# A fused hashed-attention and gated feed-forward kernel: the first head prepared in two mixed parts, a new order for the first batch, and a last output row in three parts

## The chip, the cores and the metric

The kernel runs on one core of a Trainium2 chip. The metric is the device time of one execution in microseconds (us); three executions of the kernel before the change are given, and one further execution was recorded by the profiler. A difference under 0.2% cannot be told from no change here.

## The reference

Batch 4, 8 heads, 768 positions, head width 64; q, k, v are float32. `proj` is 64x6: a position's bucket is the sign pattern of six projections.

```python
q_bits = (einsum('bhsd,dk->bhsk', q, proj) > 0); k_bits = the same of k
mask   = q_bucket[:, :, :, None] == k_bucket[:, :, None, :]
scores = where(mask, q @ k.T / sqrt(64), -1e9)
attn   = softmax(scores);  x = (attn @ v), heads side by side: 3072 x 512
g, val = x @ w_gate, x @ w_val                       # 512 x 1536 each
out    = x + sigmoid(x @ w_res) * ((gelu(g) * val) @ w_out)
```

## The kernel before, in words

The mask becomes part of the matmul. Every row of q and k (64 numbers) gets six bits (plus or minus a half) and a constant behind it, 71 numbers in all, so that one product of 71-number rows gives a score that the exponential turns to nothing where the buckets differ.

A *pair* is two heads; there are 16 pairs, four in each batch, and a batch ends with its feed-forward stage. 768 positions are six tiles of 128 (T = 6), so that a pair has twelve tiles of q and twelve of k. What one side of a pair goes through, with the short names of the lists:

- `ld`: q or k arrives by a DMA that SyncE issues (`lv`: v). The first head's q and k are loaded by themselves (L125), q0, k0, q1, k1; the rest of the first loads follow in the order FIRST_LOADS.
- `tr` (L240): VectorE transposes the float32 data in blocks of 32.
- `h` (L251; for the first pair `hoq`, `ho`, L293): TensorE multiplies by `proj`, in float32.
- `tk`, `bt` (L266, L282; for the first pair `bits_one`, L299 and L301): VectorE turns the sums back and writes the six bits into `nat`, in the bfloat16 rows that are to be transposed. For side 1 (k) of pairs 1 to 3 GpSimd does half of the four writes.
- `cs` (L208, L210): GpSimd copies q (scaled) or k into the first 64 columns of `nat`. There are four `nat` buffers, so a buffer is filled again only when the pair before the last has been transposed.
- `tp` (L320) and `td` (L329): TensorE transposes a head's six tiles into PSUM and VectorE copies them to `aug`, which the scores read. From pair 4 on `tu` (L308) does both by a transposing DMA.

The digits are pair, side (0 for q, 1 for k) and head: `td201` copies the second head of q of pair 2. On the attention side `s<n>` (L448, L459) is a unit of scores: two PSUM banks of 512 columns by TensorE and one exponential of 1024 columns on ScalarE; a pair has nine units, the fifth of which ends the first head and begins the second. `v<n>` (L421) multiplies unit n's exponentials by v, and a head ends with a small product, `preset` (L393), which adds a tiny multiple of the sum of v over the tiles, so that rows without a match come out as a mean. That sum is `vs` (L346 to L350, GpSimd), and `va` (L338) is v in bfloat16. `fin` (L372, L373) divides on VectorE and writes x. Scores have two PSUM buffers (`sc_ps`), values two (`av_ps`), and two banks serve the rest.

Batch 0's attention has no feed-forward work beside it; its 36 units and everything around them stand in a list by hand, ORDER, in which each engine takes its instructions in turn and waits for the data of the one in front. The weights of the feed-forward stage arrive by DMAs that GpSimd issues (`w0` to `w11`, L193: gate and value columns in quarters, then `w_res`, then `w_out` in thirds).

Then comes `gate_val` of batch 0: for each of twelve blocks m, eight matmuls for the gate and eight for the value (L472), a Gelu on ScalarE (L489) and a product on VectorE (L492, "hh"); BESIDE names what is issued behind block m's product: the preparation of batch 1. The gate's PSUM buffer is free when the Gelu has read it, the value's when the product has. Batches 1 to 3 follow a fixed plan by slots, with the feed-forward output (`project`, L504 to L526) between the scores. Before all this TensorE multiplies zeros (`fill`, L174) until data has come. At the very end `project` computes the last 128 rows: four matmuls for the residual gate, then the output columns in two parts, 384 columns and 128, each with twelve matmuls (L518), two VectorE steps (L521, L524) and a store (L526).

Of the kernel before, what the change touches and what calls it, by code (L numbers as in the profile page):

```python
# [16 lines left out]
FIRST_LOADS = [(1, "q"), (0, "v"), (1, "k"), (2, "q"), (2, "k"), (1, "v"), (2, "v"), (3, "k"), (3, "q")]  # L17
# [29 lines left out]
def kernel(  # L47
# [12 lines left out]
    nc = tc.nc  # L60
# [99 lines left out]
    for i in range(NN):  # L160
        blank(i, nc.vector)

# [48 lines left out]

    t32, hsum, htok = {}, {}, {}
# [23 lines left out]
    def tr(p, side, h0=0, h1=2):  # L236
        if (p, side) not in t32:
            t32[p, side] = t32_pool.tile([P, HT, 2, 32], FP32, tag="t32", name="t32")
        sl = slice(h0 * T, h1 * T)
        nc.vector.transpose(t32[p, side][:, sl].rearrange("p c h n -> p (c h n)"),  # L240
                            raw[p, side][:, sl].rearrange("p c d -> p (c d)"))

# [53 lines left out]

    def bits_one(p, side, hi):
        hs = hsum.pop((p, side, hi))
        nc.vector.transpose(hs[:, 1].rearrange("p c n -> p (c n)"),  # L299
                            hs[:, 0].rearrange("p c n -> p (c n)"))  # L300
        nc.vector.tensor_scalar(nat_of((p, side))[:, hi * T:hi * T + T, D:D + NBITS],  # L301
                                hs[:, 1, :, 0:NBITS], 0.0, 0.5, op0=ALU.is_gt, op1=ALU.subtract)
        acc_done(("hs", p, side, hi))
# [19 lines left out]
    def turned(p, side, hi, eng, t0=0, t1=T):  # L323
# [6 lines left out]
        if t1 == T:  # L330
            give((p, side, hi))
            if ("pt", p, side, hi) in accs:
                acc_done(("pt", p, side, hi))

# [163 lines left out]
    def project(b):  # L498
        hh = hidden[b]
        for t in range(T):  # L500
# [41 lines left out]
    bits_one(0, 1, 0)  # L542
    turned(0, 0, 0, nc.scalar, 0, 4)
    turn_pe(0, 1, 0)
    turned(0, 1, 0, nc.vector, 0, 2)
# [79 lines left out]
    job("tdk", lambda: turned(0, 1, 0, nc.vector, 2, T))  # L625
    job("tdq", lambda: turned(0, 0, 0, nc.vector, 4, T))
# [150 lines left out]
```

## Time and profile before

| | |
|---|---|
| three executions | 345.9, 346.1, 346.1 us (median 346.1) |
| the profiled execution | 346.07 us, of which the span of the trace is 344.4 us |
| mean granted TensorE clock | 0.998 |
| TensorE matmul busy | 333.5 us (97%) |
| VectorE, ScalarE, GpSimd busy | 191.7, 206.2, 85.6 us |
| first exponential starts, last one of batch 0 ends | 8.50 us, 46.9 us |
| batch 1's first score unit | 82.44 us |
| last VectorE step ends | 341.0 us |

Times in the views are microseconds from the start of the span. A timeline row has the start, the length, the engine, the line of the kernel, the operation, the tile written and the tile read with their shapes, and how many like instructions were merged ("x6"); in brackets stands how long the engine had been idle and what it waited for. PE is TensorE, DVE VectorE, ACT ScalarE, POOL GpSimd, and SPq the queue of DMAs that SyncE issues.

### The profile page before, as it was taken

The page shows a single profiled execution, that of the slowest core. Times are in us where ns is not written, and L with a number is a line of the kernel's source. Part 1 is how long each engine was busy: PE and PEld are TensorE (multiplying, and loading weights), DVE is VectorE, ACT ScalarE, POOL GpSimd, SP SyncE. Part 2 cuts the span into 40 slices and gives each one's busy share as a digit, 9 for nine tenths or more (in the row PEclk, how much of TensorE's full clock was granted, in tenths as well). Part 3 has the DMA queues.
Part 4 walks back from the last instruction along what each step waited for, and adds up shares of the span by engine and source line. Part 5 has one row for each costly group of instructions (what it writes and reads, how often), then busy time and mean ns, then how long its engine had stood idle before and what let it go on. Part 6 is the DMA issues. An engine that isn't in the chain of part 4 may idle for free.

```text
span 344.4 us, 7546 instructions
## 1 busy us (share of the span) xinstructions
PE 333.5 (97%) x3064; PEld 204.3 (59%) x3112; DVE 191.7 (56%) x404; ACT 206.2 (60%) x232; POOL 85.6 (25%) x162
## 2 busy tenths in 40 slices
PE   8998999999999999999999999999999999999994
PEld 4675766555666655655666665656566665566442
DVE  6979737656344856757344784747244444343333
ACT  3888972226999962224999982223999984223110
POOL 3887920317055000260043200242030000000000
PEclk9999999999999999999999999999999999999999
DMA  7959998999976743528366642725430220000022
GB/s 215 376 128 280 146 241 149 181 127 176 189 175 188 210 107 78 101 39 148 82 194 188 227 115 65 131 49 109 75 100 32 55 55 30 33 0 0 32 79 75
DMA packets 71171, 42.90 MB, mean 125 GB/s; under 512 B 49504, under 2 KB 68192, under 8 KB 71136
## 3 DMA queue, kind: packets, MB, share of 16 engines
q1 hardware_dynamic: 64720, 37.17, 44.0%
q0 software_dynamic: 6336, 5.24, 10.2%
q8 instruction: 24, 0.39, 0.5%
q14 instruction: 11, 0.09, 0.1%
q10 hardware_dynamic: 80, 0.00, 0.0%
HBM read 29.36 MB, written 6.29 MB: 104 GB/s over the span
## 4 chain that ended last, share of the span: by engine, by line
PE 90%; DVE 3%; ACT 3%; issue 1%; DMA 1%; SPq 0%; POOL 0%; DVEq 0%; ACTq 0%; POOLq 0%
PE sp L472 34%; PE fps L518 18%; PE sp L448 17%; PE av L421 9%; PE rps L504 6%; PE hs L251 3%; ACT hh L459 2%; DMA ld<-in_k_dram 1%; PE pt L320 1%; PE wps L174 1%; DVE nat L282 1%; PE hs L293 1%; DVE aug L329 1%; ACT gt L489 0%; SPq L308 0%
## 5 line engine op out<-in xcount | busy, mean ns | idle before, releaser
L459 ACT ACTIVATE e<-sp 128x1024 bf16<-128x1024 f32 x108 | 109.0, 1028 | 8.0 <-PE sp L448 2.8
L489 ACT ACTIVATE gt<-sp 128x768 bf16<-128x768 f32 x48 | 38.9, 810 | 92.8 <-PE sp L472 92.8
L448 PE MATMUL sp<-aug,aug 71*128 71x256 bf16 (+1 forms) x384 | 85.8, 325 | 2.0 <-DVE aug L329 1.6
L518 PE MATMUL fps<-wo,hh 128*128 128x512 bf16 (+2 forms) x275 | 74.6, 369 | 1.4
L492 DVE TENSOR_TENSOR hh<-gt,sp 128x768 bf16<-128x768 bf16 x48 | 45.7, 953 | 48.0 <-PE sp L472 43.9
L472 PE MATMUL sp<-x_sb,wv 128*128 128x256 bf16 (+1 forms) x378 | 70.6, 325 | 0.7 <-DVE hh L492 0.4
L472 PE MATMUL sp<-x_sb,wg 128*128 128x256 bf16 (+1 forms) x373 | 70.4, 324 | 0.7
L421 PEld LDWEIGHTS <-e 128*128 128x128 bf16 x864 | 40.2, 97 | 25.1
L472 PEld LDWEIGHTS <-wv 128*128 128x128 bf16 x384 | 37.6, 98 | 25.3 <-issue 0.6
L472 PEld LDWEIGHTS <-wg 128*128 128x128 bf16 x384 | 36.7, 98 | 26.0 <-issue 2.3
L421 PE MATMUL av<-va,e 128*128 128x65 bf16 x864 | 43.4, 193 | 0.0
L518 PEld LDWEIGHTS <-hh 128*128 128x128 bf16 x300 | 27.4, 97 | 22.5
L459 ACT ACTIVATE hh<-sp 128x1024 bf16<-128x1024 f32 x36 | 34.4, 1026 | 5.1 <-PE sp L448 5.0
L521 DVE SCALAR_TENSOR_TENSOR o<-th,fps 128x512 f32<-128x512 f32 (+2 forms) x25 | 16.7, 666 | 36.9 <-PE fps L518 30.0
L448 PEld LDWEIGHTS <-aug 71*128 71x128 bf16 x384 | 29.2, 97 | 13.0 <-issue 2.0
L346 POOL TENSOR_TENSOR v<-ldv 128x384 f32<-128x384 f32 x16 | 16.0, 999 | 64.1 <-DMA ldv<-in_v_dram 64.0
L240 DVE STREAM_TRANSPOSE t<-ld 128x768 f32<-128x768 f32 (+1 forms) x34 | 30.5, 912 | 1.6 <-DMA ld<-in_k_dram 1.4
L400 DVE COPY av<-av 128x390 f32<-128x390 f32 x24 | 13.6, 567 | 29.7 <-PE av L396 29.7
L208 POOL TENSOR_SCALAR nat<-ld 128x768 bf16<-128x768 f32 (+1 forms) x16 | 13.8, 860 | 60.1 <-DMA aug<-nat 55.4
L504 PE MATMUL rps<-wr,x_sb 128*128 128x512 bf16 x90 | 25.6, 378 | 0.3
L508 ACT ACTIVATE th<-rps 128x512 f32<-128x512 f32 x24 | 14.3, 594 | 18.5 <-PE rps L504 18.5
L210 POOL CAST nat<-ld 128x768 bf16<-128x768 f32 (+1 forms) x17 | 13.3, 783 | 39.7 <-DMA aug<-nat 38.8
(64 smaller groups left out, 242.5 us busy)
## 6 DMA issues: line engine op xcount, KB each, us to landing
ldv<-in_v_dram SPq DMA_DIRECT2D x16, 384.0 KB, 5.4
out_dram<-o SPq DMA_DIRECT2D x23, 256.0 KB, 2.0
ld<-in_q_dram SPq DMA_DIRECT2D x15, 384.0 KB, 5.6
ld<-in_k_dram SPq DMA_DIRECT2D x15, 384.0 KB, 5.2
wg<-in_moe_w_gate_dram POOLq DMA_DIRECT2D x4, 384.0 KB, 8.5
wv<-in_moe_w_val_dram POOLq DMA_DIRECT2D x4, 384.0 KB, 9.0
wo<-in_moe_w_out_dram POOLq DMA_DIRECT2D x3, 512.0 KB, 9.4
wr<-in_moe_w_res_dram POOLq DMA_DIRECT2D x1, 512.0 KB, 7.7
```

Source lines behind the costliest of these rows:

```text
L240: nc.vector.transpose(t32[p, side][:, sl].rearrange("p c h n -> p (c h n)"), raw[p, side][:, sl].rearrange("p c d -> p (c d)"))
L346: nc.gpsimd.tensor_add(v3, vs[:, :, 0:3, :], vs[:, :, 3:6, :])
L421: nc.tensor.matmul(av[p, hi][:, qt, :], e[:, off:off + P], va[:, hi, jt, 0:D + 1], start=first, stop=(p >= HP and jt == T - 1), skip_group ...
L448: nc.tensor.matmul(sp[:, off:off + nq * P], ks[0:KA, hi * T + jt, :], qs[0:KA, hi * T + qt0:hi * T + qt0 + nq, :], start=True, stop=True)
L459: nc.scalar.activation(e, sp, AF.Exp, scale=float(ALPHA))
L472: nc.tensor.matmul(sp[:, c0:c1], w[:, kk, bass.ts(m, P)], xs[:, kk, c0:c1], start=(kk == 0), stop=(kk == KM - 1))
L489: nc.scalar.activation(gt, sp[:, 0:S], AF.Gelu)
L492: nc.vector.tensor_mul(hidden[b][:, m, :], gt, ps[1][:, 0:S])
L504: nc.tensor.matmul(rps, x_sb[b][:, kk, t, :], wr[:, kk, :], start=(kk == 0), stop=(kk == KM - 1))
L508: nc.scalar.activation(th, rps, AF.Tanh, scale=0.5)
L518: nc.tensor.matmul(fps[:, cs], hh[:, m, bass.ts(t, P)], wo[:, m, cs], start=(m == 0), stop=(m == KF - 1))
L521: nc.vector.scalar_tensor_tensor(o[:, cs], th[:, cs], 1.0, fps[:, cs], op0=ALU.add, op1=ALU.mult)
```

## The change

Three edits. First, the first head is no longer prepared as "q, then k" but as two parts: part 0 has tiles 0 to 3 of q and tiles 0 and 1 of k (what the first score unit reads), part 1 the other two tiles of q and four of k. Each part has a load for each side, a `t32` tile, a hash bank, one `bits_one` for both its sides, and rows of its own in a new tile `lead`; `PARTS` lists (side, first tile, end); `load_part` issues one DMA of those tiles and `turned_part` copies as `turned` does. `tpB` transposes part 1 (into a values bank), `tdk` and `tdq` copy it. The multiplications by zero are cut from 7 x 512 + 256 + 2 x 256 columns to 6 x 512 + 128, and VectorE makes two of the four copies of `proj`. Second, FIRST_LOADS, ORDER and BESIDE stand in a new order. Third, the last rows' output columns go in three parts, 256, 128 and 128, the last in a values bank.

```diff
-FIRST_LOADS = [(1, "q"), (0, "v"), (1, "k"), (2, "q"), (2, "k"), (1, "v"), (2, "v"), (3, "k"), (3, "q")]
+FIRST_LOADS = [(1, "q"), (0, "v"), (1, "k"), (2, "q"), (2, "k"), (2, "v"), (3, "q"), (1, "v"), (3, "k")]
...
 ORDER = """
-trq trk s0 tdq tdk hoq bo0 ho bo1 s1 tr10 s2 tr11 tp011 td011a td011b tp001 v0 td001 v1 s3 h00 h01
-s4 cs21 h02 h03 s5 tr20 ld41 ld40 s6 v2 v3 v4 tr21 s7 tk0 bt10 bt11 tp100 tp110 td100 td110 cs20 s8
-ld50 tp111 s9 tr30 tr31 tp101 td101 fin00 s10 lv3 v5 v6 v7 v8 fin01 s11 va1 vs1 lv4 va2 s12 ld60 h10
-h11 h12 h13 ld61 td111 s13 cs31 v9 s14 v10 v11 v12 s15 cs30 tk1 bt20 bt21 tp210 s16 td210 tp200
-td200 v13 fin10 bt31 s17 ld51 va4 v14 s18 tr50 tp201 w0 w1 w2 bt30 td201 s19 v15 vs2 s20 tp211 cs41
-td211 s21 v16 v17 cs40 s22 tr61 v18 v19 tr40 w3 s23 va3 tp310 td310 tr60 s24 v20 tp300 td300 ld70
-s25 vs3 v21 tp301 td301 s26 vs4 fin11 s27 v22 v23 fin20 tr41 s28 v24 v25 s29 tp311 td311 s30 v26
-fin21 lv6 s31 lv5 cs50 v27 s32 cs51 v28 v29 s33 xt2 v30 tr51 s34 w4 w5 w6 v31 fin30 s35 gelu v32 v33
-v34 g0 v35 fin31 g1 xt3 h20 h21 h22 w7 op40
+trq trk s0 tpB tdk tdq hoq bo0 ho s1 bo1 tr10 ld50 s2 tr11 tp011 td011a cs21 tp001 v0 td001 v1 tr20
+s3 h00 h01 td011b s4 s5 ld41 tr21 h02 h03 v2 s6 v3 s7 lv3 v4 ld51 tk0 bt10 bt11 tp100 tp110 td100
+td110 s8 tp111 ld40 va2 s9 tr30 tp101 td101 tr31 fin00 s10 td111 v5 v6 v7 v8 fin01 vs1 s11 s12 h10
+h11 h12 h13 s13 s14 cs20 va1 v9 v10 v11 s15 tk1 bt20 bt21 tp200 td200 tp210 td210 s16 v12 cs31 w0 w1
+w2 va3 tp211 cs41 s17 bt30 td211 v13 bt31 s18 vs3 tp201 fin10 s19 cs30 v14 v15 s20 v16 s21 v17 ld61
+v18 tr41 td201 s22 lv4 va4 cs40 ld60 tr40 tr50 s23 v19 tp310 vs2 fin11 td310 s24 tp300 td300 s25
+tr60 tp301 ld70 s26 v20 v21 s27 w3 v22 v23 fin20 lv5 s28 v24 s29 tp311 td311 cs51 lv6 v25 s30 td301
+v26 v27 fin21 s31 tr61 w4 s32 v28 v29 v30 cs50 vs4 w5 s33 xt2 w6 s34 tr51 v31 fin30 s35 gelu v32 v33
+v34 op40 g0 v35 fin31 g1 xt3 h20 h21 h22
...
 BESIDE = [
-    "h23 tk2 bt41",
-    "tu41 cs61 bt40",
-    "bt50",
-    "tu40 cs60 ld71 tr71",
-    "tr70",
-    "tu50 bt51 w8 w9",
-    "",
-    "w10",
-    "h30 h31 h32 h33 tu51 cs71 tk3 bt60 bt61 tu60 tu61",
-    "pr40 rp40 bt71 tu71",
-    "bt70",
-    "w11 cs70 tu70",
+    "h23 w7 tk2 bt41",
+    "bt51 tu51",
+    "tu41 cs61 bt40 tu40 cs60",
+    "tr70",
+    "bt50",
+    "",
+    "pr40 rp40",
+    "w8 w9 w10 w11 tu50 cs70 ld71 tr71 cs71",
+    "",
+    "h30 h31 h32 h33 tk3 bt60 bt61 tu61",
+    "bt71 tu71 bt70 tu70",
+    "tu60",
...
-    load_head(0, 0, 0, nc.sync)
+    PARTS = (((0, 0, 4), (1, 0, 2)), ((0, 4, T), (1, 2, T)))
...
+    for part in PARTS[0]:
+        load_part(*part)
     nc.scalar.dma_start(projn, proj.rearrange("(h r) n -> r h n", r=32))
-    load_head(0, 1, 0, nc.sync)
+    for part in PARTS[1]:
+        load_part(*part)
     load_head(0, 0, 1, nc.sync)
     load_head(0, 1, 1, nc.sync)
...
+    lead = const.tile([P, 2, T, KA + 1], BF16, name="lead")
+    for i in range(2):
+        for side in range(2):
+            d0, d1, _, _ = part_of(i, side)
+            nc.gpsimd.memset(lead[:, i, d0:d1, D + NBITS:KA], 1.0 if side == 0 else -NBITS / 4.0)
...
+    def tr_part(i, side):
...
+        nc.vector.transpose(t32[0, i][:, d0:d1].rearrange("p c h n -> p (c h n)"),
+                            raw[0, side][:, t0:t1].rearrange("p c d -> p (c d)"))
+    def hash_part(i, side):
+        if (0, i, 0) not in hsum:
+            acc(("hs", 0, i, 0))
+            hsum[0, i, 0] = av_ps.tile([P, 2, T, 32], FP32, tag="av", name="hs1")
...
+        for dh in range(2):
+            nc.tensor.matmul(hsum[0, i, 0][:, 0, d0:d1], projs[:, dh, :], t32[0, i][:, d0:d1, dh, :],
+                             start=(dh == 0), stop=(dh == 1))
     def bits_one(p, side, hi):
...
+        dst = lead[:, side] if (p, hi) == (0, 0) else nat_of((p, side))[:, hi * T:hi * T + T]
...
+    def turn_part(i, sides, av=False):
...
+            pt = av_ps.tile([P, T, P], BF16, tag="av", name="pt")
...
+            for t in range(d0, d1):
+                nc.tensor.transpose(pt[0:KA, t, :], lead[:, i, t, 0:KA], ident)
...
-            for k0, k1 in ((0, 3), (3, 4)) if last else ((0, KM),):
+            for k0, k1 in ((0, 2), (2, 3), (3, 4)) if last else ((0, KM),):
                 cs = slice(k0 * P, k1 * P)
-                if b < B - 1:
+                if last and k1 == KM:
+                    fps = av_ps.tile([P, DMODEL], FP32, tag="av", name="fps")
+                elif b < B - 1:
...
-    fill(7)
-    fill(1, 256)
+    fill(6)
+    fill(1, 128)
     spread(lambda a: projs[32 * a:32 * a + 32, :, 32 * a:32 * a + NBITS],
-           (nc.gpsimd, nc.scalar, nc.scalar, nc.gpsimd))
+           (nc.gpsimd, nc.scalar, nc.vector, nc.vector))
+    for i, side in ((0, 0), (0, 1), (1, 0)):
+        tr_part(i, side)
+        hash_part(i, side)
+    cast_part(0, 0, nc.scalar)
+    cast_part(0, 1, nc.gpsimd)
     for side in range(2):
-        tr(0, side, 0, 1)
-        hash_one(0, side, 0, av_ps, "av")
-    cast(0, 0, nc.scalar, 0, 1)
-    cast(0, 1, nc.gpsimd, 0, 1)
+        aug[0, side] = aug_pool.tile([P, HT, P], BF16, tag=f"aug{side}", name=f"aug{side}")
     bits_one(0, 0, 0)
-    turn_pe(0, 0, 0)
-    fill(2, 256)
+    tr_part(1, 1)
+    turn_part(0, (0,))
+    turn_part(0, (1,))
+    hash_part(1, 1)
+    cast_part(1, 0, nc.gpsimd)
+    cast_part(1, 1, nc.gpsimd)
+    turned_part(0, 0, nc.scalar)
+    turned_part(0, 1, nc.vector)
     bits_one(0, 1, 0)
-    turned(0, 0, 0, nc.scalar, 0, 4)
-    turn_pe(0, 1, 0)
-    turned(0, 1, 0, nc.vector, 0, 2)
     for side in range(2):
         cast(0, side, nc.gpsimd, 1, 2)
     cast(1, 0, nc.gpsimd)
...
         job(f"vs{p}", lambda p=p: vals_s(p))
     job("trq", lambda: tr(0, 0, 1, 2))
     job("trk", lambda: tr(0, 1, 1, 2))
-    job("tdk", lambda: turned(0, 1, 0, nc.vector, 2, T))
-    job("tdq", lambda: turned(0, 0, 0, nc.vector, 4, T))
+    job("tdk", lambda: turned_part(1, 1, nc.vector))
+    job("tpB", lambda: turn_part(1, (0, 1), True))
+    job("tdq", lambda: turned_part(1, 0, nc.vector))
     job("hoq", lambda: hash_one(0, 0, 1, av_ps, "av"))
     job("ho", lambda: hash_one(0, 1, 1, av_ps, "av"))
...
```

More of the change, by code (lines that the diff above doesn't have):

```diff
@@ L210, in cast, with cast_part @@
             eng.tensor_copy(dst, raw[x][:, sl])
+    def cast_part(i, side, eng):
+        d0, d1, t0, t1 = part_of(i, side)
+        dst, src = lead[:, i, d0:d1, 0:D], raw[0, side][:, t0:t1]
+        if eng is nc.scalar:
+            nc.scalar.activation(dst, src, AF.Copy, scale=(1.0, 1.0 / C)[side == 0])
+        elif side == 0:
+            eng.tensor_scalar(dst, src, 1.0 / C, 1.0, op0=ALU.mult, op1=ALU.mult)
+        else:
+            eng.tensor_copy(dst, src)
     t32, hsum, htok = {}, {}, {}
@@ L333, in turned, with turned_part @@
                 acc_done(("pt", p, side, hi))
+    part_left, part_pt = {}, {}
+    def turn_part(i, sides, av=False):
+        what = ("part", i, sides)
+        if av:
+            acc(what)
+            pt = av_ps.tile([P, T, P], BF16, tag="av", name="pt")
+        else:
+            pt = mm_ps.tile([P, T, P], BF16, tag=take(what), name="pt")
+        part_left[what] = len(sides)
+        for side in sides:
+            d0, d1, _, _ = part_of(i, side)
+            for t in range(d0, d1):
+                nc.tensor.transpose(pt[0:KA, t, :], lead[:, i, t, 0:KA], ident)
+            part_pt[i, side] = (pt, what)
+    def turned_part(i, side, eng):
+        d0, d1, t0, t1 = part_of(i, side)
+        pt, what = part_pt[i, side]
+        dst, src = aug[0, side][0:KA, t0:t1, :], pt[0:KA, d0:d1]
+        if eng is nc.scalar:
+            nc.scalar.activation(dst, src, AF.Copy)
+        else:
+            eng.tensor_copy(dst, src)
+        part_left[what] -= 1
+        if part_left[what] == 0:
+            give(what)
+            if what in accs:
+                acc_done(what)
     def vals_a(p):
```

13 lines of the change are left out of this document (12 added, 1 removed).

## The prediction

> **What bounds the kernel.** I read the chain by engine first, then a table of busy time by stage, then ScalarE's timeline, whose gaps mark where batch 0 waits.
>
> ```profile
> PE 90%; DVE 3%; ACT 3%; issue 1%; DMA 1%; SPq 0%; POOL 0%; DVEq 0%; ACTq 0%; POOLq 0%
> ```
>
> Busy time by stage (PE, PEld, DVE, ACT, POOL), cut at the first scores, at the gap spoken of below, at the start of the feed-forward stage and at batch 1:
>
> ```profile
> 7.86:33.30 25.44, 24.01 (x325) 16.83 (x325) 22.37 (x53) 21.22 (x22) 20.05 (x40) 1.00 0.86 266
> 33.30:47.00 13.70, 13.47 (x210) 10.20 (x211) 9.81 (x18) 13.20 (x15) 11.56 (x19) 1.00 1.28 190
> 47.00:82.40 35.40, 34.63 (x265) 20.65 (x268) 22.35 (x52) 11.78 (x16) 9.79 (x15) 1.00 1.01 157
> ```
>
> ScalarE's exponentials in batch 0:
>
> ```profile
> 8.50 1.02 ACT L459 ACTIVATE hh<-sp 128x1024 bf16<-128x1024 f32 x1 [1.04 <-PE sp L448]
> 10.44 1.94 ACT L459 ACTIVATE hh<-sp 128x1024 bf16<-128x1024 f32 x2 [0.92 <-PE sp L448]
> ...
> 33.78 13.16 ACT L459 ACTIVATE hh<-sp 128x1024 bf16<-128x1024 f32 x14 [1.37 <-PE sp L448]
> ```
>
> TensorE sets the time. Up to 33.3 it is busy 24.01 of 25.44 us, so a new order can win back at most 1.43 there; VectorE is nearly as full (22.37). From 33.78 fourteen exponentials run without a gap, 0.94 each, and TensorE has 0.23 idle: there both are full. The gate stage has 0.77 idle. Nothing after batch 1 begins changes except the last row. So all that can be won lies in the start, in 1.4 us of batch 0, in under 0.8 us of the gate stage, and at the end.
>
> **The start.** VectorE's path to the second score unit s1, then TensorE's, then the third load as GpSimd meets it:
>
> ```profile
> 3.50 1.04 DVE L240 STREAM_TRANSPOSE t<-ld 128x384 f32<-128x384 f32 x2 [0.16 <-DMA ld<-in_q_dram]
> 5.55 0.40 DVE L299 STREAM_TRANSPOSE hs<-hs 128x192 f32<-128x192 f32 x1 [1.02 <-PE hs L293]
> 5.99 0.20 DVE L301 TENSOR_SCALAR nat<-hs 128x36 bf16<-128x36 f32 x1
> ...
> 7.51 0.29 DVE L329 COPY aug<-pt 71x256 bf16<-71x256 bf16 x1 [0.68 <-PE pt L320]
> 7.72 1.02 DVE L240 STREAM_TRANSPOSE t<-ld 128x384 f32<-128x384 f32 x2
> 8.67 0.57 DVE L329 COPY aug<-pt 71x256 bf16<-71x256 bf16 x2
> ```
>
> ```profile
> 1.06 3.38 PE L174 MATMUL wps<-warm 128*128 128x512 bf16 x8 [1.06 <-POOL warm L138]
> 4.24 1.93 PE L293 MATMUL hs<-t,projs 128*128 128x192 f32 x8
> ...
> 8.43 1.54 PE L293 MATMUL hs<-t,projs 128*128 128x192 f32 x8
> 9.81 1.03 PE L448 MATMUL sp<-aug,aug 71*128 71x256 bf16 x6
> ```
>
> ```profile
> 5.57 0.51 POOL L208 TENSOR_SCALAR nat<-ld 128x384 bf16<-128x384 f32 x1 [1.11 <-DMA ld<-in_q_dram]
> ```
>
> The zeros shrink from 7.5 to 6.25 times 512 columns: 3.38 x 6.25/7.5 = 2.8, ending at 3.9, when the stripe of q is transposed as well (256 columns, about 0.37 by the 0.52 of 384, from 3.50). Part 0's hash is four matmuls of 128 and four of 64 columns, half of the 1.93: 0.97, or 1.3 at the slow rate of the first ones (the same eight took 1.54 later). So bits begin at about 5.4, like today's 5.55, but for q and k at once. They end at 6.05; VectorE transposes part 1's k (0.38), copies part 0's k at about 6.8 (0.29), writes part 1's bits (0.65 behind its hash, to 7.9), transposes head 1 (1.02, overlapped) and copies part 1 (0.57): 9.26, where the same copies end at 9.24 now. The first scores come some 0.5 us earlier, which is worth nothing while the next unit does not follow. And it does not: head 1's second hash `ho` now needs the values bank in which `tpB` laid part 1, and waits for `tdq`; s1 stands behind it. 9.26 plus 0.77 (half of 1.54) is 10.05 against 9.81: **0.25 late**. Bounds: 0.2 early if the hash runs at the full rate; 0.7 late if the third load, here a stripe of q, arrives at 5.5 as the third does now (`tr_part(1, 0)` stands ahead of part 0's bits on VectorE). I take 0.25 because a stripe has a third of the bytes of that load. VectorE's two copies of `proj` hide in its 0.16 of idle time and would cost at most that; GpSimd's casts and small memsets hide in its 1.11.
>
> The Trainium skill ("TensorE: Matmul & The Clock Gate", What's actually happening) says that the array runs at half rate until a free-running window of about 3.4 us has been busy; the 1.93 against 1.54 agrees. By it, a shorter run of zeros with a gap behind it could end the half rate a window later; that is a rival below.
>
> **Batch 0's list.** The rows around the 1.37 gap:
>
> ```profile
> 23.29 0.58 DVE L266 STREAM_TRANSPOSE ht<-hs 128x384 f32<-128x384 f32 x1 [0.80 <-PE hs L251]
> 23.90 1.24 DVE L282 TENSOR_SCALAR nat<-ht 32x72 bf16<-32x72 f32 x6
> 25.98 0.55 DVE L329 COPY aug<-pt 71x768 bf16<-71x768 bf16 x1 [0.83 <-PE pt L320]
> 26.81 0.55 DVE L329 COPY aug<-pt 71x768 bf16<-71x768 bf16 x1 [0.28 <-PE pt L320]
> ...
> 28.07 0.90 DVE L282 TENSOR_SCALAR nat<-ht 32x72 bf16<-32x72 f32 x2
> ...
> 29.98 2.21 DVE L282 TENSOR_SCALAR nat<-ht 32x72 bf16<-32x72 f32 x4
> 32.22 1.02 DVE L329 COPY aug<-pt 71x768 bf16<-71x768 bf16 x2
> ```
>
> ```profile
> 24.02 2.09 POOL L282 TENSOR_SCALAR nat<-ht 32x72 bf16<-32x72 f32 x4 [1.10 <-DVE ht L266]
> ...
> 28.62 0.98 POOL L193 DMA_DIRECT2D wg<-in_moe_w_gate_dram  x1
> ...
> 31.10 1.02 POOL L346 TENSOR_TENSOR v<-ldv 128x384 f32<-128x384 f32 x1
> ...
> 33.17 0.82 POOL L210 CAST nat<-ld 128x768 bf16<-128x768 f32 x1
> ```
>
> The gap stands ahead of s22, which needs all of pair 2's copies; the last end at 33.24, 9.95 behind the start of `tk1` (the first row). The new list has the same VectorE work between these two points: `tk1`, six bit writes (1.24), six more (bt30 and bt31, 0.90 + 2.21 = 3.11), four copies, `fin10` and one `tr`. Less the waits of 0.83 and 0.28 it takes 8.84. Now `td200` and `td210` stand together behind `tp200 tp210`, which TensorE reaches only behind s15: I put one wait of 0.6 there. With `tk1` at 23.5 (TensorE is full until then and carries some 0.2 of the late s1 along) the copies end at 23.5 + 8.84 + 0.6 = 32.94: **0.3 early**, if the second six bit writes again cost 3.11 and not 1.24. They cost that because they ran from 28.07 to 32.19 beside GpSimd's copy, its three weight DMAs and its add (the 28.62 and 31.10 rows). In the new list GpSimd is as full beside them (cs31, w0 to w2, va3, cs41), so I keep 3.11; at 1.24 the whole gap would go, some 1.25 less the late start, and a longer blocking could cost 0.3.
>
> The Trainium skill ("SBUF — State Buffer", Who interferes with whom) says that a VectorE operation of this kind and GpSimd share a port pair by an exclusive lock. The trace agrees, with 3.11 against 1.24, and by the rule the new neighbours are no better.
>
> Next comes GpSimd itself. `vs2` used to be done by 33.17; it now stands behind four bit writes (2.09, from 0.73 behind the start of `tk1`, 24.2), six casts (cs31, va3, cs41, cs30, va4, cs40, at 0.82), w0 to w2 (2.48, from 28.62 to 31.10) and vs3 (2.07, from 31.10 to 33.17), and takes 2.07 itself: 13.6 in all, done at 37.8 or a little later. `preset` in v22 needs it, and s28 is queued behind v22 on TensorE, which would reach v22 at about 37.7 and waits up to 0.3. So s28's exponential starts at 39.2, against 33.78 + 6 x 0.94 = 39.4 now, and **0.2 us** is left of the list, the late start included. From there eight exponentials set the pace as before. The other shifts are covered: pair 1's v, loaded later, is wanted at 24; `op40` falls into idle VectorE time; the weights come before their blocks.
>
> **The gate stage.** A product that waits behind a transposition:
>
> ```profile
> 62.10 0.98 DVE L240 STREAM_TRANSPOSE t<-ld 128x768 f32<-128x768 f32 x1 [1.36 <-DMA ld<-in_k_dram]
> ```
>
> ```profile
> 62.11 1.46 PE L472 MATMUL sp<-x_sb,wg 128*128 128x512 bf16 x8
> 63.97 1.46 PE L472 MATMUL sp<-x_sb,wv 128*128 128x512 bf16 x8 [0.39 <-DVE hh L492]
> 65.26 1.46 PE L472 MATMUL sp<-x_sb,wg 128*128 128x512 bf16 x8
> ```
>
> ```profile
> 57.91 0.89 SPq L107 DMA_DIRECT2D ld<-in_k_dram  x1
> ```
>
> ```profile
> 73.33 0.95 DVE L492 TENSOR_TENSOR hh<-gt,sp 128x768 bf16<-128x768 bf16 x1 [1.65 <-PE sp L472]
> ```
>
> `ld71` is issued at 57.91, the transposition behind it gets its data at 62.10, and TensorE's value matmuls start 1.86 behind the gate's instead of 1.29: 0.57 lost. In the new BESIDE both stand at m = 7, but SyncE passes `tu50` as soon as bt50 of m = 4 is written (about 64.1) and issues `ld71` at some 65.7: at 4.2 us it lands at 69.9, and VectorE asks for it at 70.8, with 1.65 of idle time ahead of each product to lay the 0.98 in. The stall goes; I count **0.5**, since four weight loads are issued at about 65 and may slow it. `bt71` and `bt70` together (1.95) at m = 10 put the last product 0.3 late; batch 1's first scores and four matmuls lie over it.
>
> **The last row.**
>
> ```profile
> 337.14 2.78 PE L518 MATMUL fps<-wo,hh 128*128 128x384 bf16 x24
> ```
>
> ```profile
> 339.34 0.56 DVE L521 SCALAR_TENSOR_TENSOR o<-th,fps 128x384 f32<-128x384 f32 x1 [1.40 <-PE fps L518]
> ...
> 340.41 0.28 DVE L521 SCALAR_TENSOR_TENSOR o<-th,fps 128x128 f32<-128x128 f32 x1
> 340.72 0.29 DVE L524 SCALAR_TENSOR_TENSOR o<-o,x_tok 128x128 f32<-128x128 f32 x1
> ```
>
> TensorE's 4 x 128 columns are the same, some 0.65 for each 128 (a quarter of 2.6, the 2.78 without the last one's latency). Now the second part's steps wait for the first's, which end at 340.49, and are done at 341.02. With 256 columns in front VectorE starts 0.65 earlier, 338.69; its two steps, at 0.42 between 0.28 and 0.56, end at 339.57, the next two at 340.1, and the last 128 columns' two (their matmuls are in at 340.03) at 340.65: **0.37** less. One more store is issued, in time that SyncE has. Bounds: 0.3 to 0.45, as the 256 columns cost.
>
> **The sum.** 346.07 (the profiled execution, 344.4 of it span; the median of the runs is 346.1) - 0.2 - 0.5 - 0.37 = 345.0. Its own range, by these bounds, is 344.5 to 345.4.
>
> **Rivals.** *Slower: `tr71` waits again.* Eight matmuls of each kind make a block of 2.6 us, and the eighth's product must start by 72.5, so `ld71` must be there by 71.5. Behind `tu50`, beside the four weight loads, it may take what those take:
>
> ```profile
> wo<-in_moe_w_out_dram POOLq DMA_DIRECT2D x3, 512.0 KB, 9.4
> ```
>
> 65.7 + 9.4 = 75.1 is 3.6 late, TensorE stands still that long, and the time is 346.07 - 0.2 - 0.57 - 0.37 + 3.6 = 348.5; the loss begins where it lands after 72.6, and half way is 346.9. For it: the weight loads move from 61 to just before `ld71`. Against: they have no data moving yet when `tu50` and `ld71` are issued. 0.14.
>
> *More won:* the hash runs fast and the stripes come early, s1 is 0.2 early instead of 0.25 late, GpSimd's queue moves along: 0.65 instead of 0.2, 344.5; if the bit writes are also less blocked, down to 343.9. VectorE's waits in the start (1.02, 0.68) speak for it. 0.17.
>
> *The start costs more:* the third load late, 0.7 instead of 0.25, and the list only passes it on: 345.5; 0.14. With the half rate a window longer, `ho` and `hoq` would take twice 0.77, 1.5 later in all: 346.5; 0.05, since the gap is 0.2 us in four.
>
> **Chances.** The forecast has 0.50. 0.2% is 0.7 us: faster takes the forecast but for 0.04, and the better case: 0.63. Within it: both costly starts and the edge of the others, 0.23. Slower: the late `ld71`, 0.14. The range runs from 343.8 to 346.7; it leaves out most of the slower case.
>
> **What would show it.** s1's matmuls at 10.05 (9.81 now), first exponential before 8.1; `tk1` near 23.5; the bit writes near 28 still at 0.4 to 1 us each; the gap ahead of s22 at or under 1.2 us; GpSimd's `vs2` ending near 38 with v22's `preset` behind it; no 1.86 between gate and value matmuls; the last VectorE step 0.37 closer to TensorE's last matmul. Wrong it is if s1 comes before 9.6, if `preset` never waits, or if a gate block is longer than 2.7 us around m = 8.

## The result: 0.9% slower, and the profile after

The changed kernel takes 349.18 us (median of four executions, 348.42 to 349.92) where the kernel before takes 346.1: the ratio is 1.0086, 95% interval 1.0068 to 1.0104. I had forecast 1.1 us less, and it is 3.1 more. In a later run of both (a_again, below) it was 347.93 against 345.93, ratio 1.0073 (1.0046 to 1.0100). The profiled execution took 349.92, its span is 348.2.

The chain by engine, then busy time by stage, cut at the same four events as before (first scores, the gap of batch 0, start of the feed-forward stage, batch 1):

```profile
PE 88%; DVE 4%; DMA 3%; ACT 2%; issue 1%; SPq 0%; POOL 0%; DVEq 0%; POOLq 0%
...
8.79:36.60 27.81, 26.80 (x339) 19.16 (x338) 23.66 (x55) 21.27 (x22) 19.81 (x38) 1.00 0.84 248
36.60:50.65 14.05, 13.69 (x202) 10.18 (x202) 9.79 (x19) 13.18 (x15) 11.77 (x21) 1.00 0.98 187
50.65:87.05 36.40, 34.91 (x270) 20.65 (x268) 21.60 (x49) 11.79 (x16) 11.77 (x20) 1.00 0.90 151
```

The first stage begins 0.93 later and lasts 2.37 longer (27.81 against 25.44), with TensorE busy 2.8 more on nearly the same work: it works slower, it does not wait more. The granted clock is 1.00 in these rows and in those before, so the rate is read from the durations below. The gate stage lasts 1.00 longer, and there TensorE does wait (1.49 idle where 0.77 was). The start on TensorE and VectorE, and ScalarE's first use of q's first load:

```profile
1.06 2.85 PE L194 MATMUL wps<-warm 128*128 128x512 bf16 x7 [1.06 <-POOL warm L147]
4.45 2.80 PE L340 MATMUL hs<-t,projs 128*128 128x128 f32 x12 [0.54 <-DVE t L277]
...
8.79 1.06 PE L525 MATMUL sp<-aug,aug 71*128 71x512 bf16 x2
9.80 0.82 PE L395 MATMUL pt<-ident,lead 128*71 128x128 bf16 x6
10.42 2.87 PE L330 MATMUL hs<-t,projs 128*128 128x192 f32 x8
13.09 1.22 PE L525 MATMUL sp<-aug,aug 71*128 71x256 bf16 x6
```

```profile
3.35 0.48 DVE L188 COPY projs<-projn 32x12 f32<-32x12 f32 x2
3.86 0.83 DVE L277 STREAM_TRANSPOSE t<-ld 128x256 f32<-128x256 f32 x3
```

```profile
3.27 0.42 ACT L236 ACTIVATE lead<-ld 128x256 bf16<-128x256 f32 x1
```

`hoq` and `ho` (L330) take 2.87 where they took 1.54, a score unit's two matmuls 1.06 instead of 0.60, six transpositions 0.82 instead of 0.50. All of TensorE's work up to 13.09 runs at half its later rate; before, the rate changed at 5.0, inside the first hash. s1 starts 3.28 later. Ahead of the first hash TensorE is idle for 0.54: the shorter zeros end at 3.91, and VectorE copies `proj` twice (0.48) before it transposes, although the data is there (ScalarE reads the same part of q from 3.27 on).

Batch 0 behind it, VectorE from `tk1` on and ScalarE from s22 on:

```profile
26.67 0.58 DVE L303 STREAM_TRANSPOSE ht<-hs 128x384 f32<-128x384 f32 x1 [0.68 <-PE hs L288]
27.29 1.26 DVE L319 TENSOR_SCALAR nat<-ht 32x72 bf16<-32x72 f32 x6
29.28 1.02 DVE L376 COPY aug<-pt 71x768 bf16<-71x768 bf16 x2 [0.73 <-PE pt L367]
30.33 3.14 DVE L319 TENSOR_SCALAR nat<-ht 32x72 bf16<-32x72 f32 x4
33.48 0.55 DVE L376 COPY aug<-pt 71x768 bf16<-71x768 bf16 x1
34.05 0.40 DVE L319 TENSOR_SCALAR nat<-ht 32x72 bf16<-32x72 f32 x2
...
36.08 0.51 DVE L376 COPY aug<-pt 71x768 bf16<-71x768 bf16 x1
```

```profile
37.12 8.47 ACT L536 ACTIVATE hh<-sp 128x1024 bf16<-128x1024 f32 x9 [1.30 <-PE sp L525]
45.91 4.69 ACT L536 ACTIVATE hh<-sp 128x1024 bf16<-128x1024 f32 x5 [0.32 <-ACT hh L536]
```

From `tk1` to the last copy for s22 it is 9.92, as in the profile before (9.95); a gap of 0.32 is new. The gate stage's late load, as SyncE, VectorE and TensorE show it:

```profile
69.54 0.92 SPq L107 DMA_DIRECT2D ld<-in_k_dram  x1
```

```profile
77.18 0.98 DVE L270 STREAM_TRANSPOSE t<-ld 128x768 f32<-128x768 f32 x1 [2.35 <-DMA ld<-in_k_dram]
```

```profile
76.20 1.46 PE L549 MATMUL sp<-x_sb,wg 128*128 128x512 bf16 x8
79.05 1.46 PE L549 MATMUL sp<-x_sb,wv 128*128 128x512 bf16 x8 [1.38 <-DVE hh L569]
...
87.09 0.60 PE L525 MATMUL sp<-aug,aug 71*128 71x512 bf16 x2
```

The value's matmuls start 2.85 behind the gate's instead of 1.30: 1.55 lost, where the kernel before lost 0.57 once. And the last row on VectorE:

```profile
343.54 0.42 DVE L600 SCALAR_TENSOR_TENSOR o<-th,fps 128x256 f32<-128x256 f32 x1 [0.76 <-PE fps L597]
...
345.17 0.29 DVE L603 SCALAR_TENSOR_TENSOR o<-o,x_tok 128x128 f32<-128x128 f32 x1
```

Between these events, against the same ones before:

| stretch | forecast | this execution |
|---|---|---|
| to s1 | +0.25 | +3.28 |
| s1 to the end of batch 0's last exponential (46.94; now 50.60) | -0.45 | +0.38 |
| from there to batch 1's first scores | -0.5 | +0.99 |
| from there to the end of the last VectorE step (341.01; now 345.46) | -0.37 | -0.20 |
| from there to the end of the span | 0 | -0.63 |
| sum | -1.07 | +3.82 |

### The profile page after: what moved, and what is told of

It is laid out like the page before. It is cut to its first block, busy times and chain, and to the rows that moved or that the text cites. A ratio compares the mean times of both kernels' runs of the same rounds, so it can differ in the third digit from the quotient of the medians.

```text
span 348.2 us, 7641 instructions
## 1 busy us (share of the span) xinstructions
PE 340.3 (98%) x3129; PEld 208.8 (60%) x3129; DVE 193.4 (56%) x410; ACT 205.9 (59%) x231; POOL 86.3 (25%) x167
## 3 DMA queue, kind: packets, MB, share of 16 engines
q0 software_dynamic: 6336, 5.24, 10.2%
## 4 chain that ended last, share of the span: by engine, by line
PE 88%; DVE 4%; DMA 3%; ACT 2%; issue 1%; SPq 0%; POOL 0%; DVEq 0%; POOLq 0%
PE sp L549 32%; PE fps L597 18%; PE sp L525 17%; PE av L498 9%; PE rps L581 6%; PE hs L288 3%; DMA ld<-in_k_dram 2%; ACT hh L536 2%; DMA aug<-nat 1%; PE hs L340 1%; DVE nat L319 1%; PE pt L367 1%; PE hs L330 1%; DVE aug L376 1%; PE pt L395 0%
## 5 line engine op out<-in xcount | busy, mean ns | idle before, releaser
L597 PE MATMUL fps<-wo,hh 128*128 128x512 bf16 (+2 forms) x312 | 79.6, 362 | 0.0
L549 PE MATMUL sp<-x_sb,wv 128*128 128x512 bf16 (+1 forms) x384 | 70.9, 326 | 1.4 <-DVE hh L569 1.4
L549 PE MATMUL sp<-x_sb,wg 128*128 128x512 bf16 (+1 forms) x384 | 71.0, 326 | 0.1
L597 PEld LDWEIGHTS <-hh 128*128 128x128 bf16 x312 | 28.1, 97 | 21.8
L270 DVE STREAM_TRANSPOSE t<-ld 128x768 f32<-128x768 f32 (+1 forms) x32 | 29.7, 935 | 2.4 <-DMA ld<-in_k_dram 2.4
L228 POOL TENSOR_SCALAR nat<-ld 128x768 bf16<-128x768 f32 (+1 forms) x16 | 14.5, 908 | 64.3 <-DMA aug<-nat 63.1
L581 PE MATMUL rps<-wr,x_sb 128*128 128x512 bf16 x96 | 27.1, 379 | 0.0
L319 DVE TENSOR_SCALAR nat<-htp 32x72 bf16<-32x72 f32 x96 | 21.9, 228 | 1.8
## 6 DMA issues: line engine op xcount, KB each, us to landing
wo<-in_moe_w_out_dram POOLq DMA_DIRECT2D x3, 512.0 KB, 12.8
```

Of the source, the lines that this page charges most:

```text
L319: engs[a % len(engs)].tensor_scalar(nat_of(x)[32 * a:32 * a + 32, :, D:D + NBITS], ht[32 * j:32 * j + 32, :, NBITS * a:NBITS * (a + 1)], 0 ...
L549: nc.tensor.matmul(sp[:, c0:c1], w[:, kk, bass.ts(m, P)], xs[:, kk, c0:c1], start=(kk == 0), stop=(kk == KM - 1))
L581: nc.tensor.matmul(rps, x_sb[b][:, kk, t, :], wr[:, kk, :], start=(kk == 0), stop=(kk == KM - 1))
L597: nc.tensor.matmul(fps[:, cs], hh[:, m, bass.ts(t, P)], wo[:, m, cs], start=(m == 0), stop=(m == KF - 1))
```

## The experiments

### Is it the half rate? Zeros lengthened, shortened, moved

Run a_long_zeros, on the changed kernel:

```diff
-    fill(6)
-    fill(1, 128)
+    fill(8)
```

> The changed kernel with eight matmuls of 512 zero columns ahead of the first hash instead of six and a quarter of that width, so that the zeros end at about 4.48 (1.06 + 8 x 0.427) where the first transposition of q is done, and no 0.54 of idle time is left between them. Theory A (the array's half rate, prolonged because the zeros stop 0.54 us before the hash): the matmuls go over to the full rate near 5 us as in the kernel before, the part's hash takes 1.5 instead of 2.8, `hoq` and `ho` 1.5 instead of 2.87, s1's matmuls start at 10.0 to 10.4 instead of 13.09, and the time is 349.2 - 2.8 = 346.4 (346.0 to 346.8). Theory B (the stripes' order costs it, by the wait of `ho` for the bank that part 1 uses and by VectorE's order): the rate of the matmuls may change, but s1 stays at 12.5 or later and the time at 348.5 to 349.5.

347.62 (346.93 to 348.17, twelve executions), ratio 1.0037 (1.0022 to 1.0052). Its profiled execution has no idle time ahead of the first hash and is at the full rate from there on:

```profile
4.45 1.52 PE L340 MATMUL hs<-t,projs 128*128 128x128 f32 x12
...
8.64 1.85 PE L330 MATMUL hs<-t,projs 128*128 128x192 f32 x8
10.32 1.03 PE L525 MATMUL sp<-aug,aug 71*128 71x256 bf16 x6
```

s1 comes where theory A had it, but the ratio falls only from 1.0086 to 1.0037, some 1.7 us and not 2.8, and 1.3 of loss remains.

Run b_short_zeros gives the kernel before the changed kernel's zeros:

```diff
-    fill(7)
-    fill(1, 256)
+    fill(6)
+    fill(1, 128)
```

> The kernel before with the changed kernel's zeros (six of 512 columns and one of 128 instead of seven and one of 256) and nothing else changed: they end at 3.70, and the first hash can start at 4.03. Theory A: the half rate lasts at least one 3.4 us stretch longer, so the first hash takes 2.5 instead of 1.93 and, if it lasts to 8.4, s1 starts 1 to 1.5 later, if to 12 or 13, 2 to 3 later; time 347.0 to 349.0. Theory B: the zeros are not what costs, time 346.1 within 0.3.

346.81, ratio 1.0015 (0.9999 to 1.0031): at most a little slower. Its hash takes 2.49 instead of 1.93 and s1 starts at 10.19. So short zeros alone don't make the 3 us; both theories as I wrote them were too simple. A hint lies in the kernels that have the start of before unchanged: their first hash takes 1.53 (run b_tail3, below) to 2.82 (b_best), with the same instructions.

Next, the changed kernel again, and two variants of it:

> The changed kernel once more, as the base of the next two, and to see whether the half rate lasts as long in a second profiled execution. Theory A1 (the stretches by which the rate is decided begin at another time in each execution, and one is good only if it holds no idle time of TensorE): the change to the full rate comes anywhere from 8 to 14, s1 between 11 and 13.4, time 349.2. Theory A2 (the rate depends only on how much was computed since the start): the change comes at 13.3 again.

```diff
+    late = const.tile([P, P], BF16, name="late")
+    nc.gpsimd.memset(late, 0.0)
...
-            nc.tensor.matmul(wps[:, 0:cols], warm, warm[:, 0:1].to_broadcast([P, cols]), start=True, stop=True)
+            nc.tensor.matmul(wps[:, 0:cols], late, late[:, 0:1].to_broadcast([P, cols]), start=True, stop=True)
...
-    fill(1, 128)
+    fill(1, 256)
```

> The changed kernel with nearly the same amount of zeros (six matmuls of 512 columns and one of 256, 2.77 us), but of a second tile that GpSimd clears later, so that they run from about 1.7 to 4.5 and no idle time is left ahead of the first hash. Theory A1 (the gap of 0.54 is what prolongs the half rate): the change to the full rate comes between 5.1 and 8.5, s1 between 10.3 and 11.5, time 347.6 to 348, as with eight matmuls. Theory A2 (the amount of zeros decides): as in the changed kernel, s1 near 13, 349.2.

```diff
+    fill(1, 256)
     turn_part(0, (0,))
...
-    job("tpB", lambda: turn_part(1, (0, 1), True))
+    job("tpB", lambda: (fill(1, 256), turn_part(1, (0, 1), True)))
```

> The changed kernel with its short zeros and the gap of 0.54 left as they are, but a matmul of 256 zero columns ahead of part 0's transpositions and another ahead of part 1's, where its trace has idle times of 0.12 (at 7.1 and 9.7). Theory A1: even idle times as short as these spoil a stretch; from 4.45 on there is none any more, so the full rate comes between 7.9 and 11.3, s1 at 10.6 to 12.3, time 0.7 to 2 below the unchanged one. Rival: only the 0.54 gap counts and 0.12 doesn't; no difference to the unchanged kernel beyond the 0.1 to 0.2 that the fillers take.

a_again: 347.93 (346.94 to 350.54), and its profiled execution, the fastest, with the same program as the table above:

```profile
4.31 1.52 PE L340 MATMUL hs<-t,projs 128*128 128x128 f32 x12 [0.43 <-DVE t L277]
...
10.18 1.03 PE L525 MATMUL sp<-aug,aug 71*128 71x256 bf16 x6
```

At the full rate from 4.5, with short zeros and a gap of 0.43: theory A2 falls, and the amount of zeros is no law; A1's moment (8 to 14) is missed too. a_late_zeros: s1 at 10.74 as A1 has it, but 348.54 (348.10 to 349.62), ratio 1.0078 (1.0061 to 1.0094), where A1 has at most 348. a_fill_gaps: s1 at 10.20 in this execution, but 349.22 (346.83 to 350.69), ratio 1.0090 (1.0062 to 1.0119): the fillers gain nothing that the times show, against A1's 0.7 to 2. One profiled execution of each cannot separate a cure from luck, so single executions of the unaltered kernels follow:

> The changed kernel again, one profiled execution. Theory A3 (the half rate ends at a moment that differs between executions of one and the same kernel, and this makes its spread of 3.6 us): over these looks the change to the full rate falls between 4.3 and 13.5, and each time is close to 346.9 + (s1 - 10.18), where 346.9 and 10.18 are the last profiled execution's. Theory A4 (the spread comes from later stages, the transfers above all): s1 is within 0.5 of 10.2 in each, and the times differ all the same.

> As the look before: time within 0.4 of 346.9 + (s1 - 10.18) by theory A3; by A4 s1 is near 10.2 whatever the time.

> A third look at the changed kernel, with the same two expectations: 346.9 + (s1 - 10.18) within 0.4 by theory A3, s1 near 10.2 by A4.

> The kernel before, one profiled execution. Theory A3: its half rate ends between 4.2 and 7.1, as in the seven executions with the same start so far, and never later, since its first zeros, hash and transpositions leave no idle time in that stretch; s1 between 9.4 and 10.7, time 346.1 + (s1 - 9.81) within 0.4. Theory A4: s1 at 9.8 whatever the time.

| execution | s1's matmuls start | time | time less s1 |
|---|---|---|---|
| changed, first profile | 13.09 | 349.92 | 336.83 |
| a_again | 10.18 | 346.94 | 336.76 |
| a_look1 | 12.91 | 349.85 | 336.94 |
| a_look2 | 12.97 | 350.67 | 337.70 |
| a_look3 | 12.82 | 350.68 | 337.86 |
| before, first profile | 9.81 | 346.07 | 336.26 |
| b_look | 10.66 | 346.68 | 336.02 |

Theory A3 holds: what an execution loses in the start it keeps to the end. The changed kernel's s1 is at 10.2 once and at 12.8 to 13.1 four times, on average 12.4; eight executions with the start of before have it at 9.42 to 10.70, on average 10.3 and never later. That is 2.1 us on average. a_look2 and a_look3 missed the 0.4 by a second step, 0.8 to 0.9 more behind s1. VectorE and ScalarE in a_look1:

```profile
18.82 1.38 DVE L319 TENSOR_SCALAR nat<-ht 32x72 bf16<-32x72 f32 x6
...
21.31 2.86 ACT L536 ACTIVATE hh<-sp 128x1024 bf16<-128x1024 f32 x3 [0.39 <-PE sp L525]
```

and in a_look2:

```profile
18.88 2.15 DVE L319 TENSOR_SCALAR nat<-ht 32x72 bf16<-32x72 f32 x6
...
22.14 2.86 ACT L536 ACTIVATE hh<-sp 128x1024 bf16<-128x1024 f32 x3 [1.16 <-PE sp L525]
```

The same six bit writes of pair 1 take 1.38 or 2.15, and the gap ahead of a later unit grows by as much. Five of thirteen profiled executions with the new list show the long form (a_look2, a_look3, b_new_list, a_late_zeros and the run a_fill_gaps), none of seven with the old one. Part of a_late_zeros' time is this: its time less s1 is 337.74.

What prolongs the half rate? In the late executions TensorE has two more idle times of some 0.16, ahead of part 0's and of part 1's transpositions. The views give no wait there; I read them from the distance of the starts (0.38 behind the last hash matmul, where such matmuls follow each other by 0.21). Two more executions of the kernel that fills them:

> The kernel with the two fillers of 256 columns again, one profiled execution. In four of five executions of the changed kernel the rate changed 3.1 to 3.5 us behind the last idle time ahead of `tpB` (0.16 at 9.5; another of 0.16 stands at 6.9). Theory A5 (each idle time, even of 0.16, starts the count anew): with the fillers there is none behind 4.4, so in an execution that isn't fast at 4.5 already the rate changes between 7.5 and 8.5, and s1 comes at 10.6 to 11.5. Rival A6 (idle times as short as these don't count): the rate changes at 12.6 or later again, s1 near 13.

> The same kernel in a second execution, with the same expectations: where it isn't fast at 4.5 already, the full rate between 7.5 and 8.5 and s1 at 10.6 to 11.5 by theory A5, s1 near 13 by A6.

The second was at the full rate early (s1 at 10.26, 347.19). The first was not:

```profile
4.31 2.80 PE L340 MATMUL hs<-t,projs 128*128 128x128 f32 x12 [0.40 <-POOL lead L238]
6.90 0.42 PE L194 MATMUL wps<-warm 128*128 128x256 bf16 x1
...
9.39 0.27 PE L194 MATMUL wps<-warm 128*128 128x256 bf16 x1
...
11.90 1.03 PE L525 MATMUL sp<-aug,aug 71*128 71x256 bf16 x6
```

The first filler still takes 0.42, the second 0.27: the rate changed at about 9.2, not at 12.6 or later, and s1 comes at 11.90. That speaks against A6, though the rate changes 0.7 later than A5's range and s1 comes 0.4 later; it is one execution. The Trainium skill ("TensorE: Matmul & The Clock Gate", What's actually happening) says that the window over which activity is counted runs freely and does not begin with the kernel, so that the moment of change varies by some 500 ns. The traces agree that it varies with nothing changed, but by far more. Twelve profiled executions have no idle time ahead of the first hash, or 0.15 (b_short_zeros): the eight with the start of before, b_short_zeros, a_long_zeros, a_late_zeros and a_weights_apart (below). In all of them the rate changes between 4.2 and 7.1. Eight have an idle time of 0.40 to 0.55 there: the changed kernel's five and the three with fillers. In three of them the rate changes by 4.5, in five only at 9.2 to 13.3. So only executions with that gap are late, though not all of them. The times agree: those of a_long_zeros and a_late_zeros lie within 1.2 and 1.5, those of a_again and a_fill_gaps, which have the gap, within 3.6 and 3.9. What the two of 0.16 add, and how long a gap may be, is not settled. No run takes VectorE's copies back by themselves.

### The lists by themselves

Run b_new_list is the kernel before with the new FIRST_LOADS, ORDER and BESIDE; b_order_only has the first two of them, and `w7` at the end of ORDER, where the old BESIDE wants it. In both the beginning of the new ORDER is fitted to the old start (the rest of its first line is left out here):

```diff
-trq trk s0 tpB tdk tdq hoq bo0 ho s1 bo1 tr10 ld50 s2
+trq trk s0 tdq tdk hoq bo0 ho bo1 s1 tr10 ld50 s2
```

> The kernel before with its own start and its own last row, but with the changed kernel's list for batch 0, its side list of the gate stage and its order of loads. Theory L (the list and the side list lose by themselves what the trace of the changed kernel shows behind s1: 0.4 up to the last exponential, 1.0 in the gate stage, 0.2 behind it): 346.1 + 1.6 = 347.7, with 1.5 of waiting for `ld71` ahead of a value block. Theory P (they lose there only because the start is 3 late, so that transfers and the order no longer fit): 346.1 - 0.45 - 0.5 = 345.2, no block later than its neighbours.

> The kernel before with the changed kernel's list for batch 0 and order of first loads, and its own start, gate stage side list and last row. Theory L1 (the list by itself costs what stands between s1 and the last exponential in the changed kernel, 0.3 to 0.4, or up to 0.9 as with the whole new list): 346.4 + 0.3 to 0.9, 346.7 to 347.3. Theory P (the prediction's: it gains 0.45 by itself): 345.9. What the gate stage then loses is 0.6, as in the kernel before.

b_new_list: 350.81 (348.96 to 353.84), ratio 1.0132 (1.0095 to 1.0170), worse than the whole change. The gate stage of its profiled execution, the slowest of the six, on TensorE:

```profile
74.14 1.46 PE L472 MATMUL sp<-x_sb,wg 128*128 128x512 bf16 x8
79.51 2.72 PE L472 MATMUL sp<-x_sb,wv 128*128 128x512 bf16 x8 [3.91 <-DVE hh L492]
82.16 2.79 PE L251 MATMUL hs<-t,projw 128*32 128x192 f32 x32
```

`ld71` took 10.1 us from issue to landing here (7.6 in the changed kernel, 4.2 before), TensorE stood still for 3.91, and then worked at half rate again: 2.72 instead of 1.46, 2.79 instead of 1.51. This execution loses 6.1 between batch 0 and batch 1 (41.6 against 35.5). The late load is theory L's; its price, 1.6 in all, is a third of the 4.4 measured, and the half rate behind the wait was not in it. Why the load takes longer here than in the changed kernel stays open.

b_order_only: 346.82 (346.61 to 347.28), ratio 1.0026 (1.0016 to 1.0037), so the gain of 0.45 is refuted. Its trace has 37.18 from s1 to the last exponential's end (37.13 before), with bit writes of 3.14 and 0.40 as above, and its time less s1 is 336.40 (336.26 and 336.02 before). So 0.1 to 0.4 of its 0.9 lies behind s1 in this execution. The other traces say more of the list: from s1 to the last exponential's end the seven executions with the old ORDER take 36.61 to 37.16 (mean 36.9), the thirteen with the new one 37.18 to 37.66 where the bit writes of pair 1 are short and 38.04 to 38.28 where they are long. The profile before, with 37.13, is at the upper end of the old ones. Where the rest of the 0.9 comes from I leave open.

Then the load. Run a_weights_apart is a_long_zeros with

```diff
-    "h23 w7 tk2 bt41",
+    "h23 w7 w8 w9 tk2 bt41",
...
-    "w8 w9 w10 w11 tu50 cs70 ld71 tr71 cs71",
-    "",
+    "tu50 cs70 ld71 tr71 cs71",
+    "w10 w11",
```

> The changed kernel with the eight zero matmuls, and with the four weight loads taken away from the load `ld71`: w8 and w9 are issued at the start of the gate stage, w10 and w11 one block behind `ld71`, which stays where it is. Theory W (the load is late because it shares the array of DMA engines with the weight loads and stands behind a transposing transfer that they slow): `ld71` takes 4.2 us as in the kernel before instead of 7.5, lands by 71, the wait of 1.24 ahead of a value block goes, and the time is 347.6 - 1.5 = 346.1 (345.7 to 346.5). Theory Q (it is late because `tu50` stands ahead of it on SyncE, with or without weights): it still lands at 73 or later and the time stays at 347.6.

346.25 (345.36 to 347.45), ratio 1.0002 (0.9986 to 1.0017) where a_long_zeros has 1.0037. SyncE and VectorE:

```profile
67.52 0.90 SPq L107 DMA_DIRECT2D ld<-in_k_dram  x1
```

```profile
71.86 0.95 DVE L569 TENSOR_TENSOR hh<-gt,sp 128x768 bf16<-128x768 bf16 x1 [1.20 <-PE sp L549]
72.73 0.97 DVE L270 STREAM_TRANSPOSE t<-ld 128x768 f32<-128x768 f32 x1
74.46 0.95 DVE L569 TENSOR_TENSOR hh<-gt,sp 128x768 bf16<-128x768 bf16 x1 [0.76 <-PE sp L549]
```

The load lands 4.8 after its issue (0.6 more than theory W has, but in time), the transposition waits for nothing, and no value block is late. From the last exponential to batch 1 it is 34.94, where a_long_zeros has 36.34. Theory W holds: the four weight loads beside the load cost 1.4 us. Without them the new BESIDE does what the prediction wanted of it, since the kernel before takes 35.50. s1 starts at 11.15 in this execution, with the same start as in a_long_zeros (10.32).

### The last row, and a better kernel

The kernel before with the last row as in the change:

```diff
-            for k0, k1 in ((0, 3), (3, 4)) if last else ((0, KM),):
+            for k0, k1 in ((0, 2), (2, 3), (3, 4)) if last else ((0, KM),):
...
+                if last and k1 == KM:
+                    fps = av_ps.tile([P, DMODEL], FP32, tag="av", name="fps")
```

> The kernel before with only the last output row in three column parts. The last VectorE step ends 0.37 earlier, as the two traces show behind the last full row (3.76 in before, 3.38 in after). Theory P (what the prediction said): the time falls by 0.37, to 345.7. Theory E (SyncE's waits at the end run through eight semaphores in a fixed order, some 0.06 each, and one store more moves the last store one place on in that order): 0.37 + 0.06, 345.65. The 0.98 by which the changed kernel's stretch from the last VectorE step's predecessor row to the end is shorter in all would come here only if the last store moved as far in the order as there.

345.39 (344.63 to 346.37), ratio 0.9982 (0.9967 to 0.9997): a gain. The interval holds both expected sizes. The trace has the last step's end 0.38 closer to the last full row's, as in the changed kernel; from the last step to the end of the span it is 3.18 (3.35 before, 2.72 in the changed kernel). On top of that, `tr71` one block later:

```diff
-    "tu40 cs60 ld71 tr71",
-    "tr70",
+    "tu40 cs60 ld71 tr70",
+    "tr71",
```

> The kernel before with the last row in three parts, and with the transposition `tr71` put one block later in the gate stage's side list, behind `tr70`, so that VectorE does not wait for `ld71` ahead of a product. Theory G (the prediction's step: the wait costs 0.57 and nothing takes its place): 345.4 - 0.57 = 344.8, and no block of matmuls is later than its neighbours. Theory N (the next step becomes late instead): 345.4, the wait seen one block further on.

344.66 (343.94 to 345.77), ratio 0.9963 (0.9949 to 0.9977), the lowest median of all. From the last exponential to batch 1 it is 34.95 where it was 35.50, and no block is late: theory G.

Two last runs are for the 0.63 behind the last step, which I had not foreseen. Both cut the stores of two full rows of the last batch into four each, of other rows (b_best has `T - 5 <= t < T - 3`):

```diff
+                parts = KM if b == B - 1 and T - 3 <= t < T - 1 else 1
...
-                nc.sync.dma_start(out_t[b, t][:, cs], o[:, cs])
+                    nc.sync.dma_start(out_t[b, t][:, c0:c1], o[:, c0:c1])
```

> The same kernel with the stores of two full rows of the last batch each cut into four column parts, six stores more, so that the last store of all falls on the last of the eight semaphores that SyncE waits for at the end instead of the second. Theory E: behind the last landing there are then one or two waits of 0.06 instead of seven, 1.1 us instead of 1.6 from the last landing to the end, so 0.4 to 0.6 less than the kernel without it, 344.3. Rival: the waits at the end are not what the end stands on, no difference within 0.2.

> The kernel before with the last row in three parts, `tr71` one block later, and the stores of two full rows of the last batch cut in four, this time the fourth and fifth row from the end, so that SyncE is free when the last steps' stores are to be issued (with the second and third from the end it was 0.44 late with the last one). Theory E: from the last landing to the end 0.9 instead of 1.6 without anything else later: 0.7 below the kernel without the six stores, 344.0. Rival (the waits at the end do not count): 344.7.

345.19, ratio 0.9974 (0.9962 to 0.9985), and 344.85, ratio 0.9967 (0.9953 to 0.9981): neither is faster than the kernel without. In the trace b_best has 2.90 from the end of the last VectorE step to the end of the span, against 3.18 without the cut stores and 2.72 in the changed kernel; part of what the waits lost came back as a later last store. Times cannot decide it, since s1 alone moves 1.3 between executions.

## Why the prediction was wrong, point by point

- **The start** is the step that failed. I had priced the half rate as a rival at 346.5 and gave it 0.05, "since the gap is 0.2 us in four". The gap is 0.40 to 0.55 in the five executions: VectorE's two copies of `proj`, which were to "hide in its 0.16 of idle time and would cost at most that", take 0.34 to 0.48 and push the transposition from 3.50 to 3.72 or 3.86. The price was wrong too. I counted only `ho` and `hoq` at half rate, 1.5; the first hash (2.80 instead of 1.52), part 1's hash and both sets of transpositions run at it as well, 2.9 between a_again and the first profile. And I read the 1.93 of the old hash as a property of the kernel, while it is one draw of 1.53 to 2.82.
- **s1 at 10.05** is right where the rate is full: 10.18, first exponential at 7.90. But at the full rate the old start has s1 at 9.42, so the parts lose 0.76, not 0.25. That `tpB` and the wait for the bank, which stand ahead, make the difference is argued, not shown.
- **The list** gains nothing. My 0.51 behind `tk1` is 0.03: the second six bit writes cost 3.54 and not 3.11, and the wait for TensorE 0.73 and not 0.6. That they would again be blocked was right. The 3.11 was a draw too: with the old list the first two of these writes take 0.40 to 0.93 and the gap ahead of s22 0.86 to 1.40, with the new one always 1.29 to 1.32. `preset` in v22 did not wait for `vs2`, one of the signs I had named against me. The new 0.32, which b_order_only and b_new_list do not have, and, in some executions, 0.8 at pair 1's bit writes were nowhere in the sum.
- **The gate stage** is the slower rival (0.14) and not the forecast: the stall did not go, it grew from 0.57 to 1.55. SyncE issued `ld71` at 69.54, and 65.7 plus the shift of 3.66 is 69.4, so that step was right. The wrong one is that the four weight loads, with "no data moving yet", would leave it at 4.2 us; it took 7.6. The rival's own 9.4 was too long here and about right in b_new_list. It names two moments from which the load costs time, 71.5 and 72.6; landing at 77.1, or 73.5 without the shift, the load cost 1.55, which puts the moment at about 71.9.
- **The last row** is right, 0.38 against 0.37, though batches 1 to 3 lost some 0.2 of it in this execution. The end of the kernel gave 0.6 more, of which the three parts by themselves, in b_tail3, give 0.2.

On average over the profiled executions, then: the half rate and the parts' order some 2.1 (the s1 of both kernels), the list 0.6 or, with the long bit writes, 1.4, the gate stage 1.0, and the end 0.8 back. a_long_zeros takes off most of the rate's share, a_weights_apart the load's as well, and no difference to the kernel before is left.

## What to carry to other kernels

Work that only keeps TensorE busy should reach to the first real matmul: an idle time of 0.40 to 0.55 ahead of it came with a late full rate in five of eight executions, and none of the twelve with at most 0.15 was late. Whatever is put ahead of that matmul on another engine (here two small copies on VectorE) can open such a gap. A duration at the start of one profile may be a draw: look at several executions before it goes into a sum. A load that a transposition needs soon should not be issued beside bulk loads that could go a few blocks earlier or later.

## What the runs showed of the hardware that I had not expected

TensorE's half rate ended anywhere from 4.2 to 13.3 us, with one and the same program by 4.5 and at 13.3. An idle time of 3.91 us in mid-kernel brought it back for the next two groups of matmuls (2.72 and 2.79 instead of 1.46 and 1.51); one of 1.38 did not. Six bit writes of one form on VectorE took 1.38 or 2.15 in the same place of the same program. From the last VectorE step to the end of the span there were 3.35 us before and 2.72 after, with one more store; with that store alone (b_tail3) there were 3.18, so the store count is not the whole of it.
